# Row sums placed ten rows per head by one-hot weights, and the DMA chain to the softmax broadcast cut from nine transfers to three

## The chip, the cores and the metric

The kernel runs on one core of a Trainium2 chip. The metric is the device time of one execution in microseconds (us). Five engines work side by side, each through its own list of instructions in order: TensorE (PE, matmuls), VectorE (DVE), ScalarE (ACT), GpSimd (POOL) and SyncE (SP, which here only issues DMA transfers). They wait for each other through semaphores.

## What is computed

The reference is an attention in two parts, followed by a dense layer pair with a SiLU between:

```python
# q, k, v: [8 batches, 8 heads, 576, 64]
q_d, k_d, v_d = means of 4 neighbouring rows           # 144 rows
out_up   = repeat(softmax(q_d k_d^T / 8) v_d, 4)       # coarse part
out_local = softmax(q k^T / 8, masked to |i - j| < 4) v # band part
x = (out_up + out_local) reshaped to [4608, 512]
h = x @ w_in                                            # [4608, 2048]
out = (h * sigmoid(h)) @ w_out                          # [4608, 512]
```

Each softmax needs the sum of a row of exponentials and its reciprocal. The change is about how these sums get from TensorE to the place where the attention output is multiplied by them.

## The kernel before

Two heads make a pair; there are 32 pairs. For pair `p` the exponentials lie transposed (keys on partitions, queries along the free axis) in `Pt` (band part, 576 queries) and `Pd` (coarse part, 2 x 72 keys, 144 queries). There are five buffers of each (`NP_ = 5`), four of the broadcast reciprocals `Rb` (`NR = 4`), and two PSUM pairs `duo` for everything that attention does on TensorE.

Pairs 0 to 7 (`direct`) get their reciprocals through matmuls (`ph_ZD`, `ph_RB`). Pairs 8 to 31 use the chain that is changed, two pairs at a time (`z = p // 2`), twelve passes in all:

```python
def ph_Z(z):
    D, bk = next_duo()
    i = z % 2
    ...
    hd = [(32 * (2 * a + h), prs[a] % NP_, h) for a in range(2) for h in range(2)]
    for o, m, h in hd:                       # 4 heads, side by side in 4 column groups
        mm(D[o:o + 32, 0, 0:360], ones_bf[:, 0:32], Pt[m][:, h, 0:360], ...)
    for o, m, h in hd:
        mm(D[o:o + 32, 1, 0:216], ones_bf[:, 0:32], Pt[m][:, h, 360:576], ...)
    for s in range(2):
        for o, m, h in hd:
            mm(D[o:o + 32, 1, 216:360], fours_bf[:, 0:32], Pd[m][:, h, s, :], ...)
    # 720 sums per head, the same in each of 32 rows
    P.op("ACT", lambda e: e.activation(zc[i], D[:, :, 0:360], AF.Copy), ...)          # PSUM -> SBUF
    for o in range(4):                                                              # 4 DMAs
        P.op("SP", lambda s, o=o: s.dma_start(
            zr[i][10 * o:10 * o + 10, :],                     # one row of 720 -> ten of 72
            zsrc[32 * o:32 * o + 1, :].rearrange("p (c n) -> p c n", c=10)), ...)

def do_recip(z):
    P.op("DVE", lambda e: e.reciprocal(rr[i], zr[i]), ...)                            # 40 x 72
    P.op("SP", lambda s: s.dma_start(scr[i].rearrange(...), rr[i]), ...)              # 1 DMA, to DRAM

def do_bcast(z):
    for a in range(2):
        for h in range(2):                                                          # 4 DMAs
            P.op("SP", lambda s: s.dma_start(
                Rb[n][64 * h:64 * h + 64, :],                 # one row of 720 to 64 partitions
                scr[i][2 * a + h:2 * a + h + 1, :].to_broadcast([64, 720])), ...)

def ph_PV(p):
    ...                                                       # 14 matmuls into a duo
    P.op("DVE", ... xo[x][:, 0:456]   = D[:, 0, 0:456] * Rb[u][:, 0:456])
    P.op("DVE", ... xo[x][:, 456:720] = D[:, 1, 0:264] * Rb[u][:, 456:720])
    do_add(p)                                                 # POOL: band + coarse -> xT
```

The dense layers are cut in nine token blocks of 512. A first-layer group `g1` is four matmuls into `hps`, a tanh on ACT (`th`) and a multiply on DVE (`gT`); a second-layer group `g2` is four matmuls into `ops`. There are 144 of each.

The order of all instructions is planned in the program itself, by a list scheduler: every operation is given a duration (`cost`, in ns), every DMA an issue time and a cost on a modelled ring, and the planner takes next what would be ready first. Each engine then executes its list in that fixed order. A changed duration can therefore move instructions anywhere in the kernel.

Of the kernel before, what the change touches and what calls it, by code (L numbers as in the profile page):

```python
# [32 lines left out]
class Op:  # L33
    __slots__ = ("t0", "eng", "fn", "waits", "pos", "K", "inc", "dsem", "dval", "semval", "end")
# [7 lines left out]
class Prog:  # L42
# [9 lines left out]
    def __init__(self):  # L52
        self.streams = {e: [] for e in self.ENGS}
        self.know = {e: {} for e in self.ENGS}
        self.dcount = {}
        self.free = {e: 0 for e in self.ENGS}
        self.rings = {"SP": [], "POOL": [], "ACT": []}
        self.ring_t = 0

# [54 lines left out]
    def op(self, eng, fn, r=(), w=(), dma=None, cost=0):  # L114
        op = Op(eng, fn)
        op.pos = len(self.streams[eng])
        know = self.know[eng]
        deps = []
        for x in r:
            if x.psum:  # L120
                deps += [(o, False) for e, o in x.last.items() if e != eng]
            else:
                deps += [(o, True) for o in x.writers]
        for x in w:
            if x.psum:
                deps += [(o, False) for e, o in x.last.items() if e != eng]
            else:
                rd = x.readers + ([op] if x in r else [])
                if rd:
                    x.prev, x.readers, x.writers = rd + x.writers, [], []  # L130
                deps += [(o, dma is not None or eng != "PE") for o in x.prev]
                if dma is not None:
                    deps += [(o, True) for o in x.writers if o.dsem != dma]
        deps = [(d, f) for d, f in deps if d is not op]
        t = self.free[eng]
        for d, f in deps:
            if d.eng != eng or d.dsem:
                t = max(t, d.end + self.LATENCY[d.eng])
        if dma:
            op.t0 = t  # L140
            t += 450 if eng == "SP" else 650 if eng == "ACT" else 800
            self.free[eng] = max(t, self._dma(op, eng, t, cost * DMA_SLOW) if eng != "POOL" else t)
            if eng == "POOL":
                self._dma(op, eng, t, cost * DMA_SLOW)
        else:
            self.free[eng] = op.end = t + cost * (2 if eng == "PE" and t < 30000 else 1)
        deps.sort(key=lambda df: -(df[0].pos if not df[0].dsem else 1 << 30))
        for d, f in deps:
            self._dep(op, d, know, f)
        op.waits = [  # L150
            w for w in op.waits
            if not any(v is not w and v[2].K.get(w[0], -1) >= w[1] for v in op.waits)
        ]
        for x in r:
            if x.psum:
                x.last[eng] = op
            elif x not in w:
                x.readers.append(op)
        for x in w:
            if x.psum:  # L160
                x.last[eng] = op
            else:
                x.writers.append(op)
        op.K = dict(know)
        if dma:
            self.dcount[dma] = self.dcount.get(dma, 0) + 16
            op.dsem, op.dval = dma, self.dcount[dma]
            op.K[dma] = op.dval
        else:
            op.K[eng] = op.pos  # L170
        self.streams[eng].append(op)
        return op
# [36 lines left out]
def bass_hourglass_attn__then__act_silu_kernel(  # L209
# [9 lines left out]
    with kctx:  # L219
# [40 lines left out]
        zc = sb("zc", [128, 2, 360], F32, 2)  # L260
        zr = sb("zr", [40, 72], F32, 2)
        rr = sb("rr", [40, 72], F32, 2)
        Rb = sb("Rb", [128, 720], F32, NR)
        xo = sb("xo", [128, 720], F32, 2)
        scr = [nc.dram_tensor(f"scr{i}", [4, 720], F32, kind="Internal").ap() for i in range(2)]
# [3 lines left out]
        ones_bf = sb("ones_bf", [128, 64], BF16)  # L269
        fours_bf = sb("fours_bf", [72, 64], BF16)  # L270
# [23 lines left out]
        def const_g():  # L294
            pool(lambda g: g.memset(ones_bf[:, :], 1.0), w=[R("ones")])
            pool(lambda g: g.memset(fours_bf[:, :], 4.0), w=[R("ones")])
# [41 lines left out]
        def load_T(p, x):  # L338
            j = p % 2
            src, dst = (qb, qr) if x == "q" else (kb, kr)  # L340
            P.op("SP", lambda e: e.dma_start_transpose(
                dst[j][:, :, :], src[j][:, :, :, :].rearrange("p c h d -> p (c h d)")),
                r=[R(f"{x}b{j}")], w=[R(f"{x}r{j}")], dma=f"{x}r{j}", cost=700)
            P.free["SP"] += 700

        def order_T(p, x):
# [3 lines left out]
            if x == "q":  # L350
                P.op("DVE", lambda e: e.tensor_copy(dst, src), r=[R(f"qr{j}")], w=[R(f"qT{y}")], cost=700)
            else:
                P.op("ACT", lambda e: e.activation(dst, src, AF.Copy), r=[R(f"kr{j}")], w=[R(f"kT{y}")], cost=700)  # L353

        def load_v(p):
# [3 lines left out]
            for hh in range(2):  # L359
# [4 lines left out]
                     w=rs_, dma=sem, cost=900)  # L364
            if p in direct:
# [3 lines left out]
                 w=[R(f"vq{i}")], dma=f"vq{i}", cost=870)  # L369
            P.op("SP", lambda s: s.dma_start(vq[i][64:72, :, :], src[64:72]),  # L370
                 w=[R(f"vq{i}")], dma=f"vq{i}", cost=150)
# [104 lines left out]
        def chain(z):  # L476
            return "SP"

        def ph_Z(z):
# [5 lines left out]
            for o, m, h in hd:  # L485
                mm(D[o:o + 32, 0, 0:360], ones_bf[:, 0:32], Pt[m][:, h, 0:360], rr_, [bk[0]],
                   cost=40, m="col4")
            for o, m, h in hd:
                mm(D[o:o + 32, 1, 0:216], ones_bf[:, 0:32], Pt[m][:, h, 360:576], rr_, [bk[1]],
                   cost=24, m="col4")  # L490
            for s in range(2):
                for o, m, h in hd:
                    mm(D[o:o + 32, 1, 216:360], fours_bf[:, 0:32], Pd[m][:, h, s, :], rr_, [bk[1]],
                       start=(s == 0), stop=(s == 1), cost=16, m="col4")
            P.op("ACT", lambda e: e.activation(zc[i][:, :, :], D[:, :, 0:360], AF.Copy),
                 r=bk, w=[R(f"zc{i}")], cost=770)
            zsrc = zc[i][:, :, :].rearrange("p a n -> p (a n)")
            for o in range(4):
                P.op(chain(z), lambda s, o=o: s.dma_start(  # L499
                    zr[i][10 * o:10 * o + 10, :], zsrc[32 * o:32 * o + 1, :].rearrange("p (c n) -> p c n", c=10)),  # L500
                    r=[R(f"zc{i}")], w=[R(f"zr{i}")], dma=f"zr{i}", cost=100)

        def do_recip(z):
            i = z % 2
            P.op("DVE", lambda e: e.reciprocal(rr[i][:, :], zr[i][:, :]), r=[R(f"zr{i}")], w=[R(f"rr{i}")],
                 cost=600)
            P.op(chain(z), lambda s: s.dma_start(
                scr[i].rearrange("h (c n) -> (h c) n", c=10), rr[i][:, :]),
                r=[R(f"rr{i}")], w=[R(f"scr{i}")], dma=f"scr{i}", cost=100)

        def do_bcast(z):
            i = z % 2
            for a in range(2):
                n = (2 * z + a) % NR
                for h in range(2):
                    P.op(chain(z), lambda s, a=a, h=h, n=n: s.dma_start(
                        Rb[n][64 * h:64 * h + 64, :],
                        scr[i][2 * a + h:2 * a + h + 1, :].to_broadcast([64, 720])),
                        r=[R(f"scr{i}")], w=[R(f"Rb{n}")], dma=f"Rb{n}", cost=500)
# [26 lines left out]
        def const_neg():  # L546

            t = zc[1][:, 0, 0:32].rearrange("p (a g) -> p a g", a=2)
            for a in range(2):
                pool(lambda g, a=a: g.memset(t[:, a, :], -1.0), w=[R("zc1")])  # L550
                for sign, base in ((1, -1 - a), (-1, 7)):
                    pool(lambda g, a=a, sign=sign, base=base: g.affine_select(
                        out=t[:, a, :], in_=t[:, a, :], compare_op=ALU.is_ge, fill=0.0, base=base,
                        pattern=[[-8 * sign, 16]], channel_multiplier=sign), r=[R("zc1")], w=[R("zc1")], cost=120)
            P.op("DVE", lambda e: e.tensor_reduce(neg[:, :], t, mybir.AxisListType.X, ALU.add),
                 r=[R("zc1")], w=[R("neg")], cost=120)
# [22 lines left out]
        def ph_ZD(p):  # L579
# [8 lines left out]
            for s in range(4):  # L588
                for t in range(2):
# [10 lines left out]
            P.op("DVE", lambda e: e.tensor_copy(b0, f0), r=rf, w=rb, cost=150)  # L600
            P.op("DVE", lambda e: e.scalar_tensor_tensor(f1, b0, neg[:, 0:1], f0, ALU.mult, ALU.add),
                 r=rf + rb + [R("neg")], w=rf, cost=150)
            P.op("DVE", lambda e: e.tensor_copy(b1, f1), r=rf, w=rb, cost=150)
            P.op("DVE", lambda e: e.scalar_tensor_tensor(b2, b1, neg[:, 1:2], f1, ALU.mult, ALU.add),
                 r=rf + rb + [R("neg")], w=rb, cost=150)
# [136 lines left out]
        def nm(k, p):  # L742
# [8 lines left out]
            (f"dm{x}", lambda x=x: const_d(x)) for x in range(6)]  # L751
# [5 lines left out]
        for p in range(NPAIR):  # L757
# [34 lines left out]
            elif p % 2 == 1:  # L792
                task(side, f"r{z}", "DVE", [f"Z{z}"], [R(f"zr{z % 2}")], [], lambda z=z: do_recip(z))
                task(side, f"b{z}", chain(z), [f"r{z}", nm("PV", p - 1 - NR), nm("PV", p - NR)],
# [20 lines left out]
            elif p % 2 == 1:  # L815
                task(attn, f"Z{z}", "PE", [f"k{p - 1}", f"k{p}"],
# [18 lines left out]
        def run_side(now, horizon):  # L835

            nxt, again = None, True
            while again:
                again, nxt = False, None
                for t in side[:90]:  # L840
# [4 lines left out]
                    if tm <= now + horizon:  # L845
                        side.remove(t)
                        done.add(t[0])
                        t[5]()
# [35 lines left out]
        const_g()  # L884
        done.add("ones")
        while attn or side or g2n[0] < 16 * NSUP:
# [10 lines left out]
            if ready:  # L897
# [3 lines left out]
                done.add(t[0])  # L901
                t[5]()
                last = t[0]
            elif mready:
# [6 lines left out]
                else:  # L911
                    want = mready[0][1]
                run_mlp(want)
# [43 lines left out]
```

## Time and profile before

The median of 3 runs is 409.66 us (409.6 to 410.45). The profiled execution has a span of 409.0 us and a mean granted TensorE clock of 0.966 of full speed.

| Chain to the broadcast, per pass of two pairs | instructions | duration of one (us) |
|---|---|---|
| copy `zc<-duo` on ACT (L495) | 1 | 0.77 |
| DMA `zr<-zc`, issue on SP (L499) | 4 | 0.73 (median) |
| reciprocal on DVE (L505), 40 x 72 | 1 | 0.59 |
| DMA `scr<-rr`, issue on SP (L507) | 1 | 0.36 (median) |
| DMA `Rb<-scr`, issue on SP (L516), 180 KB each | 4 | 0.60 (median), 4.0 from issue to landing |

How to read the page: PE is TensorE's matmuls and PEld its weight loads, which overlap them; SPq is SP's queue of DMA issues. Rows of 40 digits cut the span in 40 equal slices; a digit is a busy share in tenths, and in the row PEclk the granted clock in tenths. L499 is line 499 of the program. The chain of waits starts at the last instruction and goes back, at each step, to what released it. In a table by stretches, each engine's busy us stand beside the stretch's length, with the number of instructions in brackets; behind them stand the granted clock, the mean busy share of the 16 DMA engines, and GB/s. In a timeline, a line is start, length, engine, source line and instruction, and in square brackets the idle time before it with what ended it.

### The profile page before, as it was taken

What the parts mean: (1) busy time and instruction counts of PE and PEld (TensorE: products, weight loads), DVE (VectorE), ACT (ScalarE), POOL (GpSimd) and SP (SyncE); (2) the same over time, 40 slices, a digit from 0 to 9 for tenths busy, and PEclk for the clock granted to TensorE, in tenths of its full rate; (3) what the DMA queues carried; (4) which work ended last, traced back from release to release, by engine and by line L of the source; (5) the groups of instructions that cost most, each with busy time, mean ns of one, the idle gap of its engine ahead of it and who ended that gap; (6) DMA issues with size and microseconds to landing.
All of it is one profiled execution on the core that took longest, in us unless ns stands there. A gap on an engine that the chain in (4) does not pass through costs nothing.

```text
span 409.0 us, 7353 instructions
## 1 busy us (share of the span) xinstructions
PE 350.3 (86%) x2891; PEld 210.9 (52%) x2928; DVE 245.0 (60%) x391; ACT 224.9 (55%) x379; POOL 161.6 (40%) x211
## 2 busy tenths in 40 slices
PE   2566977869999888779886998889998989999996
PEld 1445745536655455435542665446545555555552
DVE  3958756965777846657477577347775663343320
ACT  4564645718666783648661975455865334344331
POOL 7953713267316643960375406832614220000000
PEclk9999798989999989999988999989999999999999
DMA  8999799567787888997989886979871501101012
GB/s 222 240 315 275 130 217 208 126 155 178 170 240 154 216 194 187 220 184 188 224 210 189 192 164 191 196 194 248 149 214 57 133 14 41 38 27 51 26 53 77
DMA packets 97082, 66.50 MB, mean 163 GB/s; under 512 B 66072, under 2 KB 87320, under 8 KB 97048
## 3 DMA queue, kind: packets, MB, share of 16 engines
q1 hardware_dynamic: 92824, 59.74, 65.2%
q0 software_dynamic: 4224, 6.29, 6.9%
q8 instruction: 23, 0.38, 0.4%
q14 instruction: 11, 0.09, 0.1%
HBM read 53.67 MB, written 9.58 MB: 155 GB/s over the span
## 4 chain that ended last, share of the span: by engine, by line
PE 48%; DMA 13%; DVE 11%; SPq 10%; ACT 7%; POOL 7%; issue 3%; POOLq 0%; ACTq 0%
PE ops L413 21%; PE hps L413 20%; PE duo L413 6%; DMA vs<-in_v_dram 5%; SPq L499 3%; DMA Rb<-scr 3%; DVE gT L688 3%; ACT th L686 2%; DMA vq<-in_v_dram 2%; SPq L363 2%; DVE Pt L471 2%; ACT Pt L448 1%; DMA zr<-zc 1%; DMA kr<-kb 1%; PE duo L423 1%
## 5 line engine op out<-in xcount | busy, mean ns | idle before, releaser
L413 PE MATMUL hps<-xT,w_in_sb 128*128 128x512 f32 x576 | 175.3, 436 | 16.9 <-DVE gT L688 16.8
L688 DVE SCALAR_TENSOR_TENSOR gT<-th,hps 128x512 bf16<-128x512 f32 x144 | 97.8, 685 | 107.9 <-ACT th L686 107.5
L413 PE MATMUL ops<-w_out_bf,gT 128*128 128x512 bf16 x539 | 138.0, 385 | 5.0 <-issue 2.5
L413 PEld LDWEIGHTS hps<-xT,w_in_sb 128*128 128x128 f32 x576 | 107.9, 196 | 54.7 <-DVE gT L688 27.0
L686 ACT ACTIVATE th<-hps 128x512 f32<-128x512 f32 x144 | 85.2, 598 | 78.9 <-PE hps L413 78.5
L413 PEld LDWEIGHTS ops<-w_out_bf,gT 128*128 128x128 bf16 x576 | 48.5, 99 | 69.5 <-issue 21.8
L663 POOL TENSOR_TENSOR xT<-xo 128x576 fp32r<-128x576 f32 (+2 forms) x40 | 41.4, 1048 | 101.8 <-DVE xo L646 101.8
L385 POOL CAST qb<-qs 96x768 bf16<-96x768 f32 x28 | 25.2, 902 | 56.7 <-DMA qs<-in_q_dram 43.0
L448 ACT ACTIVATE Pt<-duo 128x912 bf16<-128x912 f32 x32 | 29.7, 928 | 12.6 <-PE duo L413 12.5
L707 ACT ACTIVATE osb<-ops 128x512 f32<-128x512 f32 x36 | 21.5, 598 | 27.1 <-PE ops L413 27.1
L394 POOL TENSOR_TENSOR vt<-vq 72x512 f32<-72x512 f32 x24 | 31.9, 1329 | 4.5 <-DMA vq<-in_v_dram 3.4
L390 ACT ACTIVATE vb<-vs 128x640 bf16<-128x640 f32 x30 | 21.8, 734 | 21.5 <-DMA vs<-in_v_dram 20.1
L471 DVE TENSOR_TENSOR Pt<-Pt,mask_bf 128x1152 bf16<-128x1152 bf16 x32 | 30.3, 949 | 5.4 <-ACT Pt L463 5.4
L644 DVE TENSOR_TENSOR xo<-duo,Rb 128x456 f32<-128x456 f32 x32 | 20.0, 624 | 12.3 <-DMA Rb<-scr 9.3
L385 POOL CAST kb<-ks 96x768 bf16<-96x768 f32 x28 | 24.1, 860 | 2.2 <-DMA ks<-in_k_dram 2.1
L413 PE MATMUL duo<-qT,kT 64*128 64x112 bf16 (+1 forms) x320 | 18.4, 230 | 7.0 <-DVE xo L644 3.0
L435 DVE TENSOR_REDUCE kd<-kT 128x144 bf16<-128x576 bf16 x32 | 23.7, 740 | 1.0 <-ACT kT L353 1.0
L435 DVE TENSOR_REDUCE qd<-qT 128x144 bf16<-128x576 bf16 x32 | 23.8, 745 | 0.5
L353 ACT ACTIVATE kT<-kr 128x576 bf16<-128x576 bf16 x16 | 19.3, 1206 | 7.9 <-DMA kr<-kb 7.9
L413 PEld LDWEIGHTS duo<-qT,kT 64*128 64x128 bf16 x320 | 10.7, 101 | 21.5 <-issue 8.3
L465 ACT ACTIVATE Pd<-duo 72x576 bf16<-72x576 f32 x32 | 20.7, 646 | 0.0
L396 POOL TENSOR_TENSOR vd<-vt 72x256 bf16<-72x256 f32 x24 | 18.7, 780 | 1.9
(68 smaller groups left out, 263.5 us busy)
## 6 DMA issues: line engine op xcount, KB each, us to landing
vs<-in_v_dram SPq DMA_DIRECT2D x60, 160.0 KB, 5.1
out_dram<-osb SPq DMA_DIRECT2D x36, 256.0 KB, 2.5
qs<-in_q_dram SPq DMA_DIRECT2D x30, 288.0 KB, 4.7
ks<-in_k_dram SPq DMA_DIRECT2D x30, 288.0 KB, 5.4
Rb<-scr SPq DMA_DIRECT2D x48, 180.0 KB, 4.0
vq<-in_v_dram SPq DMA_DIRECT2D x24, 256.0 KB
w_in_sb<-in_moe_w_in_dram POOLq DMA_DIRECT2D x4, 1024.0 KB, 11.4
w_out_bf<-in_moe_w_out_dram POOLq DMA_DIRECT2D x4, 512.0 KB, 8.8
```

The costliest lines, as they stand in the source:

```text
L385: pool(lambda g, d=dst, s=src: g.tensor_copy(d, s), r=rs_, w=[R(f"{nm}b{j}")], cost=830)
L390: P.op("ACT", lambda e: e.activation(vb[m][:, :, :], t, AF.Copy), r=rs_, w=[R(f"vb{m}")], cost=730)
L394: pool(lambda g: g.tensor_tensor(vt[:, :, :], vq[i][:, :, 0:128], vq[i][:, :, 128:256], ALU.add), r=[R(f"vq{i}")], w=[R("vt")], cost=1290)
L413: return P.op("PE", lambda t: t.matmul(out_, lhsT, rhs, start=start, stop=stop, skip_group_check=True), r, w, cost=cost)
L435: P.op("DVE", lambda e: e.tensor_reduce(dst[j][:, :], src[y][:, :].rearrange("p (g r) -> p g r", r=4), mybir.AxisListType.X, ALU.add), r=[ ...
L448: P.op("ACT", lambda e: e.activation(Pt[m][:, :, 0:456], D[:, :, 0:456], AF.Exp, scale=0.125), r=bk, w=[R(f"P{m}")], cost=930)
L465: P.op("ACT", lambda e: e.activation(Pd[m][:, :, :, :].rearrange("p h s n -> p h (s n)"), D[0:72, :, 120:408], AF.Exp, scale=0.0078125), r ...
L471: P.op("DVE", lambda e: e.tensor_tensor(Pt[m][:, :, :], Pt[m][:, :, :], mask_bf[:, :].unsqueeze(1).to_broadcast([128, 2, S_]), ALU.mult), ...
L663: P.op("POOL", lambda e, dst=dst, in0=in0, in1=in1: e.tensor_tensor(dst, in0, in1, ALU.add), r=[R(f"xo{x}")], w=xblk(kc, t, e_), cost=200 ...
L686: P.op("ACT", lambda e: e.activation(th[tb][:, :], hps[hb][:, :], AF.Tanh, scale=0.5), r=[R(f"h{hb}", True)], w=[R(f"th{tb}")], cost=600)
L688: P.op("DVE", lambda e: e.scalar_tensor_tensor(gT[j % 2][:, f, :], th[tb][:, :], 1.0, hps[hb][:, :], ALU.add, ALU.mult), r=[R(f"h{hb}", Tr ...
L707: P.op("ACT", lambda e: e.activation(osb[s_][:, :], ops[ob][:, :], AF.Copy, scale=0.5), r=[R(f"o{ob}", True)], w=[R(f"osb{s_}")], cost=600)
```

## The change

The aim is a shorter way from the row sums to the broadcast. TensorE now puts the 720 sums of a head into ten rows of 72 at once: for block `c` of 72 queries the weights have ones only in column `c` (and its repeats), so that the sums land in row `c` and zeros are added to the others. The reciprocal can then read PSUM directly with 72 columns; the ACT copy and the four rearranging DMAs go. The broadcast's four DMAs become two, each for one head of both pairs. The planner's durations are also changed, for DMA issues, transposes, the copy to `kT` and some DVE operations. The core of the diff:

```diff
-        zc = sb("zc", [128, 2, 360], F32, 2)
-        zr = sb("zr", [40, 72], F32, 2)
-        rr = sb("rr", [40, 72], F32, 2)
-        Rb = sb("Rb", [128, 720], F32, NR)
+        rr = sb("rr", [128, 72], F32, 2)
+        Rbz = sb("Rb", [128, 2, 720], F32, NR // 2)
+        Rb = [Rbz[u // 2][:, u % 2, :] for u in range(NR)]
-        scr = [... [4, 720] ...]
+        scr = [... [128, 72] ...]
-        ones_bf, fours_bf (two memsets on POOL, at the start)
+        onesZ = sb("onesZ", [128, 10, 32], BF16)   (two memsets, two selects on POOL, after the other constants)
...
 def ph_Z(z):
-            for o, m, h in hd: mm(D[o:o + 32, 0, 0:360], ones_bf[:, 0:32], Pt[m][:, h, 0:360], ...)
-            ... (16 matmuls in all)
-            P.op("ACT", ... zc ...)
-            for o in range(4): P.op(SP, ... zr ... DMA)
+            for c in range(12):
+                for o, m, h in hd:
+                    y, t = (c, 0) if c < 8 else (8 + (c - 8) // 2, c % 2)
+                    lhsT, rhs = ((onesZ[:, y, :], Pt[m][:, h, 72 * c:72 * c + 72]) if c < 8 else
+                                 (onesZ[0:72, y, :], Pd[m][:, h, t, 72 * (y - 8):72 * (y - 8) + 72]))
+                    mm(D[o:o + 32, 0, 0:72], lhsT, rhs, rr_, bk[0:1], start=(c == 0), stop=(c == 11), ...)
+            P.op("DVE", lambda e: e.reciprocal(rr[i][:, :], D[:, 0, 0:72]), ...)
 def do_bcast(z):
-            for a in range(2):
-                for h in range(2): ... one DMA of [64, 720]
+            for h in range(2):
+                src = bass.AP(tensor=scr[i].tensor, offset=scr[i].offset + 32 * 72 * h,
+                              ap=[[0, 64], [64 * 72, 2], [1, 720]])
+                P.op("SP", ... dma_start(Rbz[i][64 * h:64 * h + 64, :, :], src), ..., cost=1100, issue=650)
...
 planner's figures (ns)
-  every DMA issue on SP: 450; transpose: 700 on the ring and 700 of SP
+  issue 400 (scr), 550 (vs), 670 and 500 (vq), 650 (Rb), 1250 (transpose, ring 950); others 450
-  kT copy 700; the four small DVE operations of ph_ZD: 150 each
+  kT copy 1210; those four: 210, 314, 210, 314
```

## Prediction

> **What bounds the kernel now.** I read the page first: parts 1, 2 and 4, for which engine is full, when, and what the chain that ended last is made of.
>
> ```profile
> span 409.0 us, 7353 instructions
> PE 350.3 (86%) x2891; PEld 210.9 (52%) x2928; DVE 245.0 (60%) x391; ACT 224.9 (55%) x379; POOL 161.6 (40%) x211
> ...
> PE   2566977869999888779886998889998989999996
> ...
> PEclk9999798989999989999988999989999999999999
> DMA  8999799567787888997989886979871501101012
> ...
> PE 48%; DMA 13%; DVE 11%; SPq 10%; ACT 7%; POOL 7%; issue 3%; POOLq 0%; ACTq 0%
> PE ops L413 21%; PE hps L413 20%; PE duo L413 6%; DMA vs<-in_v_dram 5%; SPq L499 3%; DMA Rb<-scr 3%; DVE gT L688 3%; ACT th L686 2%; DMA vq<-in_v_dram 2%; SPq L363 2%; DVE Pt L471 2%; ACT Pt L448 1%; DMA zr<-zc 1%; DMA kr<-kb 1%; PE duo L423 1%
> ```
>
> PE is the fullest engine, but only 48% of the chain is PE. Of the rest, 23% is DMA flight and the SP queue that issues DMAs, and 3% is one issuing line, L499, the four small copies `zr<-zc`. Slices of 6 to 8 in the PE row sit mostly in the first 60% of the span, while the DMA row shows 8 and 9. So the kernel has three stages, and busy time by stretches gives their sizes:
>
> ```profile
> core 0: us, PE busy (x) PEld busy (x) DVE busy (x) ACT busy (x) POOL busy (x), PEclk, DMA share, GB/s
> 100.00:140.00 40.00, 38.88 (x362) 22.65 (x367) 30.21 (x44) 26.60 (x46) 19.06 (x22) 1.00 0.86 203
> 140.00:180.00 40.00, 32.02 (x236) 18.79 (x240) 25.85 (x44) 23.00 (x37) 23.09 (x23) 0.96 0.91 195
> 180.00:220.00 40.00, 32.85 (x227) 19.39 (x230) 25.97 (x39) 25.16 (x40) 16.35 (x19) 0.93 0.95 204
> 220.00:260.00 40.00, 37.15 (x288) 21.62 (x290) 25.96 (x42) 25.63 (x42) 17.64 (x19) 0.99 0.83 183
> ...
> 340.00:409.00 69.00, 65.54 (x289) 36.95 (x292) 21.29 (x31) 24.58 (x42) 0.00 (x0) 1.00 0.12 46
> ```
>
> From 340 us on only the MLP is left and PE is full, at 0.93 us per group of four hps matmuls and 0.88 us per group of four ops matmuls (the chain's pieces there). The change can't shorten that work. The first 100 us hold pairs 0 to 7, which are `direct` and never use the changed chain; PE is idle there about 29 us, which I leave as it is. What can move is 100 to 340 us, where the other 24 pairs run: PE idle of 1.1, 8.0, 7.1 and 2.9 us in the four stretches shown, and by the same table 2.9 in 260 to 300 and 3.7 in 300 to 340: **25.7 us**. The granted clock also dips there. In 20 us stretches it is 0.91, 0.86, 0.97 and 0.91 (from 140, 200, 220 and 260 us), so 20 x (0.09 + 0.14 + 0.03 + 0.09) = **7.0 us** of PE time. Together 32.7 us can be had at most.
>
> Why PE idles there: the chain from the row sums to the broadcast. Its last pass, in the timelines of ACT, SP and DVE (start, length, instruction):
>
> ```profile
> 313.19 0.77 ACT L495 ACTIVATE zc<-duo 128x720 f32<-128x720 f32 x1 [0.63 <-PE duo L413]
> 313.98 2.99 SPq L499 DMA_DIRECT2D zr<-zc  x4
> ...
> 319.07 0.58 DVE L505 RECIPROCAL rr<-zr 40x72 f32<-40x72 f32 x1
> 320.52 0.52 SPq L507 DMA_DIRECT2D scr<-rr  x1
> 323.48 2.36 SPq L516 DMA_DIRECT2D Rb<-scr  x4
> 328.83 0.62 DVE L644 TENSOR_TENSOR xo<-duo,Rb 128x456 f32<-128x456 f32 x1
> ```
>
> It takes 15.6 us, though there is little else on the SP queue by then. Measured in the same way for all twelve passes (start of L495 to start of the first L644 of its two pairs) it is 15.6 to 31.8 us, mean 23.5. The matrices of a pair are held in one of five `Pt` buffers until its PV matmuls, so this latency limits how fast pairs follow each other (the last 24 take 126 to 329 us, 8.5 us each). And the SP queue runs in order: from 120 to 280 us it is busy 36.9, 38.2, 37.7 and 32.4 us of each 40, by its timeline. L499 alone takes 48 x 0.73 = 35 us of it, and the loads of later pairs stand behind it.
>
> **What the Trainium skill says.** "DMA: Bandwidth & Descriptors", Anatomy of one DMA, says that a small DMA's fixed cost is mostly waiting for confirmation that its last byte has landed. The trace agrees: `scr<-rr` moves 11.2 KB, and 320.52 to 323.48 pass before the dependent issue, 3.0 us. The same page, Latency and other measured facts, says that memory latency grows under load; one 2.8 KB `zr` copy issued at 198.00 took 5.5 us on the chain, with DMA at 0.95 share. "TensorE: Matmul & The Clock Gate", The HAM clock gate, ties the clock to how busy PE has been; the trace has the lower clock (0.86) in 200 to 220 us, where PE is busy 13.5 of 20 us, so part of the 7.0 us should come back with the idle time. Its remark that small matmuls cannot start closer together than about 25 ns does not bind here: `ph_ZD`'s 48 matmuls, packed four across the array, took 44.35 to 44.95 us, 12.5 ns each.
>
> **The change part by part**, each over 12 passes.
> - ACT: the `zc` copy goes, 12 x 0.77 = 9.2 us. ACT is 55% busy; off the path, except as 0.8 us of each latency.
> - SP: 48 `zr` issues go (35 us), 24 of the 48 `Rb` issues go (24 x 0.60 = 14 us), and the larger ones left may cost a little more. I take **-48 us** of issue time, 20% of the 240 us stage.
> - DVE: the reciprocal stays, now 128x72 from PSUM. L599 does 128x90 from PSUM in 716 ns, 8.0 ns a column, so 72 columns are 0.57 us against 0.59 now: nothing.
> - PE: 16 matmuls of a pass become 48 of 72 columns. Now a pass lasts 0.49 us (104.49 to 104.98); the first 16 of `ph_ZD`, the same shape, took 0.23 us, so 48 take 0.69: **+0.2 us, 2.4 us in all**, on the path.
> - DMA bytes: the broadcast still writes 720 KB a pass; `scr` grows from 11 to 36 KB. DMA engine load stays.
> - POOL: building `onesZ` costs about 1 us near 20 us; needed only after 100 us.
> - Latency of a pass: reciprocal 0.6, `scr` issued to landed 3.0, second `Rb` issue 0.6 and its landing 4.0 (median): **8.2 us against 15.6** in the least loaded pass, so 7 us less at least, and more where four `zr` issues now queue.
> - Order: the new order of instructions is planned with issue times and durations near those measured here (1.25 us per transpose, 1.21 for the kT copy). Its PE stream has 112 hps and 101 ops groups ahead of the last PV against 107 and 98, and 5 + 6 groups between the last row sums and that PV, 5 x 0.93 + 6 x 0.88 = 9.9 us, enough to cover 8.2. The tail after the PV shrinks from 37 x 0.93 + 46 x 0.88 = 74.9 to 67.6 us. That only moves work; it gains when the gaps it fills were idle.
>
> **The sum.** By the table of waits DVE stood idle for `Rb` 9.3 us and for `zr` 6.6 us, and PE's largest wait in this stage (11.5 us, hps on gT) is for DVE, whose queue is in order behind those. 15.9 us is about half of the 32.7, and half (16.3) is what I choose: the other half belongs to q, k and v loads, casts and two-deep PSUM buffers, which stay. Less 2.4 for PE's added work: 13.9. 409.7 - 13.9 = **396 us**.
>
> **The rivals.**
> 1. *DMA takes over.* Its share is 0.83 to 0.95 from 100 to 300 us, with the same bytes to move. If 190 to 200 GB/s is all that these 256-byte pieces allow, a free SP queue only waits for a full ring. For it: single `vs` issues of over 3 us. Against: 0.86 at 100 to 140 us, and 203 GB/s beside 297 at 20 to 40 us. Only the last pass, which no load follows, would then be shorter, by 7 us: about 403.
> 2. *PE becomes the bound everywhere.* All 32.7 recovered, less 2.4: 379. The five `Pt` buffers and the casts behind loads (POOL waits 43 us for `qs`) speak against it.
> 3. *The new order collides.* A whole new order, in-order queues, and the reciprocal holding a PSUM pair until DVE comes to it. PE would show new waits on rr, and the time be 405 to 412 (nothing won, and PE's added 2.4 us lost). Against: its durations fit this trace better than the old ones.
>
> **Range and chances.** Between rival 1 and a recovery of three quarters of the 32.7 lies 387 to 405. The 2% line is at 401.5 us, 5.5 above my figure: three chances in four to be beyond it, and few for a loss.
>
> **What would show it.** Right: row sums to first `xo` of about 10 to 15 us on average; SP busy below 32 us per 40; PE idle in 100 to 340 us below 15; the clock nearer 1.00 there; last PV near 325 us or earlier. Wrong: DMA share pinned at 0.95 or more with `vs` or `qs` waits larger; PE waiting on rr; a first 100 us that the new order has made longer; or latency halved with PE idle unchanged, in which case loads and not this chain set the pace.

## The result, and the profile after

The changed kernel takes **394.75 us** (median of 4 runs, 390.6 to 396.44) against 410.06 (4 runs, 409.6 to 410.74): the ratio is 0.961, with a 95% interval of 0.953 to 0.969. Forecast were 396 us and 387 to 405. The profiled run is the longest of the four, 396.44 us. Its page, parts 1, 2 and 4:

```profile
span 394.7 us, 8030 instructions
PE 346.1 (88%) x3272; PEld 213.9 (54%) x3312; DVE 248.7 (63%) x391; ACT 217.6 (55%) x367; POOL 162.6 (41%) x213
...
PE   2658886959999979998999999999979999999996
...
PEclk9999696968999997999999999999989999999999
DMA  8999699865596599999999999999983031000012
...
PE 60%; DMA 12%; DVE 11%; ACT 7%; POOL 5%; issue 3%; SPq 2%; POOLq 0%; ACTq 0%; DVEq 0%
```

PE holds 60% of the chain that ended last, 48% before; the SP queue fell from 10% to 2%, and DMA flight stayed at 12%. The span is 14.3 us shorter; in PE's two parts that is idle time, 58.7 to 48.6 us (-10.1), and busy time, 350.3 to 346.1 (-4.2). Busy time by stretches, columns as in the table before:

```profile
core 0: us, PE busy (x) PEld busy (x) DVE busy (x) ACT busy (x) POOL busy (x), PEclk, DMA share, GB/s
...
100.00:140.00 40.00, 38.31 (x438) 23.82 (x445) 30.94 (x46) 25.30 (x45) 20.90 (x25) 1.00 0.71 177
140.00:180.00 40.00, 35.82 (x355) 22.57 (x357) 30.18 (x49) 27.30 (x44) 22.49 (x23) 0.91 1.19 206
180.00:220.00 40.00, 37.85 (x348) 22.68 (x351) 28.35 (x44) 26.41 (x42) 20.54 (x22) 1.00 1.17 226
220.00:260.00 40.00, 38.82 (x353) 22.88 (x358) 28.45 (x42) 25.41 (x42) 22.90 (x26) 1.00 1.15 230
260.00:300.00 40.00, 35.87 (x329) 21.34 (x334) 28.16 (x44) 25.58 (x42) 16.88 (x16) 0.96 1.01 199
300.00:340.00 40.00, 38.83 (x274) 24.71 (x278) 20.07 (x32) 16.98 (x30) 4.75 (x4) 1.00 0.17 53
340.00:394.70 54.70, 50.78 (x223) 28.25 (x225) 16.51 (x24) 19.43 (x33) 0.00 (x0) 1.00 0.12 44
```

From 140 to 220 us PE is now busy 35.8 and 37.9 us of 40, where it was 32.0 and 32.9. Over 100 to 340 us its idle time fell from 25.7 to **14.5 us**. Some records of PE are missing in these traces (539 and 536 of the 576 `ops` matmuls are there) and count as idle: the same order with all 576, in the last experiment, shows 10.4 us. The DMA share rose from 0.83 to 0.95 to about 1.15 over 140 to 260 us. The first 100 us gave nothing (idle 29.5, now 30.2), and the clock in 40 to 100 us was lower in this run, 0.80 against 0.89.

The last pass of the chain, in the timelines of DVE and SP:

```profile
312.41 0.60 DVE L498 RECIPROCAL rr<-duo 128x72 f32<-128x72 f32 x1
313.72 0.43 SPq L502 DMA_DIRECT2D scr<-rr  x1
315.57 1.23 SPq L510 DMA_DIRECT2D Rb<-scr  x2
...
322.97 0.63 DVE L636 TENSOR_TENSOR xo<-duo,Rb 128x456 f32<-128x456 f32 x1 [1.73 <-PE duo L421]
```

10.6 us from the reciprocal to the first `xo`, of 15.6 before; the bracket says that this `xo` waited last for PE, not for the broadcast. Over all twelve passes the mean is 17.8 us against 23.5. In the table of waits, from longest to shortest, these lines belong to the chain and to what stands behind it (who waited, for whom: us, times, longest):

```profile
PEld hps L421 <- DVE gT L680: 11.5, 15, 4.2
...
PE hps L421 <- DVE gT L680: 7.2, 7, 4.0
...
DVE xo L636 <- DMA Rb<-scr: 4.2, 3, 2.8
```

DVE stood idle for the chain's DMAs for 15.9 us before (`Rb` 9.3, `zr` 6.6), and for 4.2 now. PE's wait for `gT` fell from 16.8 to 7.2 us.

### The profile page after: what moved, and what is told of

It reads as the page before. It is cut to its first block, busy times and chain, and to the rows that moved or that the text cites. A ratio compares the mean times of both kernels' runs of the same rounds, so it can differ in the third digit from the quotient of the medians.

```text
span 394.7 us, 8030 instructions
## 1 busy us (share of the span) xinstructions
PE 346.1 (88%) x3272; PEld 213.9 (54%) x3312; DVE 248.7 (63%) x391; ACT 217.6 (55%) x367; POOL 162.6 (41%) x213
## 4 chain that ended last, share of the span: by engine, by line
PE 60%; DMA 12%; DVE 11%; ACT 7%; POOL 5%; issue 3%; SPq 2%; POOLq 0%; ACTq 0%; DVEq 0%
PE hps L421 28%; PE ops L421 24%; PE duo L421 7%; DMA Rb<-scr 4%; DMA vs<-in_v_dram 4%; ACT th L678 3%; DVE gT L680 2%; DVE xo L636 2%; DMA qr<-qb 2%; DMA kr<-kb 2%; DVE Pt L479 1%; DVE gT L593 1%; DVE xo L638 1%; ACT Pt L456 1%; DMA scr<-rr 1%
## 5 line engine op out<-in xcount | busy, mean ns | idle before, releaser
L421 PE MATMUL hps<-xT,w_in_sb 128*128 128x512 f32 x576 | 173.5, 435 | 7.2 <-DVE gT L680 7.2
L421 PE MATMUL ops<-w_out_bf,gT 128*128 128x512 bf16 x536 | 140.8, 390 | 7.2 <-issue 4.0
L421 PEld LDWEIGHTS hps<-xT,w_in_sb 128*128 128x128 f32 x576 | 109.2, 195 | 40.0 <-DVE gT L680 11.5
L655 POOL TENSOR_TENSOR xT<-xo 128x576 fp32r<-128x576 f32 (+2 forms) x40 | 40.4, 1032 | 108.4 <-DVE xo L638 108.4
L393 POOL CAST qb<-qs 96x768 bf16<-96x768 f32 x28 | 24.0, 856 | 39.0 <-DMA qs<-in_q_dram 25.0
L402 POOL TENSOR_TENSOR vt<-vq 72x512 f32<-72x512 f32 x24 | 33.2, 1384 | 8.8 <-DMA vq<-in_v_dram 8.0
L404 POOL TENSOR_TENSOR vd<-vt 72x256 bf16<-72x256 f32 x24 | 19.5, 814 | 1.9
```

The lines of the kernel that those rows point to most:

```text
L393: pool(lambda g, d=dst, s=src: g.tensor_copy(d, s), r=rs_, w=[R(f"{nm}b{j}")], cost=830)
L402: pool(lambda g: g.tensor_tensor(vt[:, :, :], vq[i][:, :, 0:128], vq[i][:, :, 128:256], ALU.add), r=[R(f"vq{i}")], w=[R("vt")], cost=1290)
L421: return P.op("PE", lambda t: t.matmul(out_, lhsT, rhs, start=start, stop=stop, skip_group_check=True), r, w, cost=cost)
L655: P.op("POOL", lambda e, dst=dst, in0=in0, in1=in1: e.tensor_tensor(dst, in0, in1, ALU.add), r=[R(f"xo{x}")], w=xblk(kc, t, e_), cost=200 ...
```

## The experiments

The theories: **L**, the latency of the chain costs time, because engines with lists in fixed order stand behind what waits for it; **Q**, the issue time of the SP queue did it, 48 us less; **F**, the planner's new figures did it; **D**, DMA bandwidth bounds the stage now. All ratios are to the kernel before, run on the same chip; they leave out executions more than 1.5% above the fastest of their kernel, which the medians and ranges include.

### The old chain with the planner's new figures

```diff
 kernel before
-  issue 450 for all, transpose 700 + 700, kT 700, ph_ZD 150
+  the new figures; zr issue=730, scr issue=400, Rb issue=600
```

> The kernel before with its nine-DMA chain, and the planner's new figures (its zr issues planned at 0.73 us, scr 0.40, Rb 0.60, as measured). Theory L (the latency of the chain sets the pace of the pairs): the chain is as long as before, so 404 to 410 us. Theory Q (issue time of the SP queue): the 35 us of zr issues are still there, so 404 to 410. Rival theory F (the planner's figures and the order that follows from them did it): 394 to 399.

Measured: **422.39 us**, ratio 1.026 (1.020 to 1.033), slower by 12 us. F falls in its plain form. The passes are as long as before (mean 23.4 us), and what the figures did is another order of PE: its list differs from the old one in many places, the last PV stands behind 112 hps and 108 ops groups instead of 107 and 98, and the last `xo` starts at 352.8 us instead of 329.7. In its table of waits:

```profile
PE hps L412 <- DVE gT L687: 12.9, 18, 2.0
PE duo L412 <- DVE xo L643: 12.1, 7, 5.5
...
PE duo L412 <- DVE Pt L470: 6.9, 5, 3.1
```

PE stands 12.1 us for `xo` to free a PSUM pair, 5.5 us in one case; it was 5.4 in all before. Why true durations make a worse order for the long chain is not settled; the planner chooses greedily, and nothing here tells which of its choices cost it.

### The new chain with the old figures

```diff
 changed kernel
-  the new figures
+  issue 450 for all, transpose 700 + 700, kT 700, ph_ZD 150
```

> The changed kernel with the planner's old figures (450 ns for every issue, 700 for transposes and the kT copy, 150 for the small DVE operations). Theories L and Q: the new chain works under any order, 395 to 400 us. Theory F: the order is planned on wrong durations again, 404 to 410.

Measured: **399.26 us**, ratio 0.971 (0.966 to 0.977). The chain alone wins 2.9% under the old figures, and PE idle from 100 to 340 us is 14.2 us, with no record missing. The figures may add another 1%; the intervals overlap, so that is not clear of noise.

### New sums, four broadcast DMAs; and old sums, two

```diff
 changed kernel
-  2 DMAs of [64, 2, 720], each for one head of both pairs
+  4 DMAs of [64, 720]; each pair waits for its own two
```

> The changed kernel, but the broadcast goes out as four DMAs of 180 KB instead of two of 360 KB; each pair waits only for its own two. Adds 24 issues of 0.6 us, 14 us of SP time. Theory L: the first pair's data may even land earlier, 393 to 397 us. Theory Q: 14 of the 48 us of issue time are back, about 4 us longer, 397 to 401.

Measured: 395.12 us, ratio 0.962 (0.958 to 0.966), the same as with two. The four land in 4.5 us (median), the two in 6.8, and the mean pass is 16.1 us: what the merged broadcast saves in issues it gives back in flight.

> The old row sums with the ACT copy and four zr DMAs, but the broadcast as two DMAs, with the new figures. Removes 14 us of SP issue time and 1.2 us of latency per pass against the run with the old chain and the new figures. Theory L: within 2 us of that run. Theory Q: 3 to 5 us below it. Theory F: the same as that run, near 396.

Measured: 421.61 us, ratio 1.025 (1.019 to 1.031), the same as the first experiment. Merging the broadcast is worth nothing that can be measured on either side; the one-hot sums are the change.

### One more hop in the chain

```diff
-  SP: scr[i] <- rr[i]
+  SP: pre[i] <- rr[i]          # DRAM
+  SP: scr[i] <- pre[i]         # DRAM to DRAM, 36 KB
```

> The changed kernel with one more small DMA in the chain: the reciprocals go to a second DRAM buffer first and from there to the one that is broadcast (36 KB, 0.4 us of issue each, 12 in all; the planner knows of it). Adds 3 to 5 us of latency per pass and only 5 us of SP issue time. Theory L (latency of the chain): the passes are 18 us now and were 23.5 before for 15 us of time, so 3 to 5 us of latency cost 7 to 12 us: 402 to 407. Theory Q (SP issue time): 395 to 397.

Measured: **404.77 us**, ratio 0.985 (0.980 to 0.989). The mean pass is 23.0 us, as in the kernel before, and 10 of the 15 us are lost, with only twelve small issues more. But the planner knew of the hop and made another order: PE's list leaves that of the changed kernel at 126 us, and 109 hps and 97 ops groups stand ahead of the last PV instead of 112 and 101. The 10 us are therefore the price of the latency together with the order planned for it; no run adds the hop in the changed kernel's order. Its waits:

```profile
PEld hps L422 <- DVE gT L686: 27.4, 28, 5.1
PE hps L422 <- DVE gT L686: 18.6, 16, 5.0
...
DVE xo L642 <- DMA Rb<-scr: 11.0, 5, 3.8
```

DVE waits 11.0 us for `Rb` (4.2 in the changed kernel), and PE 18.6 us for `gT` (7.2). DVE's list is in order, so it is tempting to read the second as caused by the first. The timelines of PE, DVE and ACT at PE's longest stall after 100 us show something else:

```profile
168.65 0.73 PE L422 MATMUL hps<-xT,w_in_sb 128*128 128x512 f32 x2 [2.74 <-DVE gT L686]
...
167.91 1.28 DVE L686 SCALAR_TENSOR_TENSOR gT<-th,hps 128x512 bf16<-128x512 f32 x2 [1.05 <-ACT th L684]
...
166.65 0.74 ACT L399 ACTIVATE vb<-vs 128x640 bf16<-128x640 f32 x1 [2.40 <-DMA vs<-in_v_dram]
167.29 1.07 ACT L684 ACTIVATE th<-hps 128x512 f32<-128x512 f32 x2
```

ACT stood for a v load, with the tanh behind it in its list. The next stall (1.75 us at 149.89) goes back to a DVE copy that waited for a q transpose; the longest that goes back to `Rb` is the eighth, 0.86 us at 278.90. The table follows every idle stretch of PE over 0.15 us, from 100 to 340 us, in this way, to the first DMA or PE instruction that ended a wait (us):

| PE's idle time goes back to | before | changed | extra hop |
|---|---|---|---|
| the chain's `Rb` and `zr` | 7.2 | 2.2 | 2.0 |
| v loads, q and k transposes | 6.9 | 2.9 | 9.7 |
| PE's own earlier matmuls | 8.1 | 5.1 | 5.9 |
| nothing that the trace shows | 1.9 | 3.0 | 1.7 |

What the hop lost stands in the second row. SP's list is in order as well, and SP stands 12.6 us for the hop to land (3.3 for the store in the changed kernel), but none of this falls between 130 and 260 us, where the loss is: PE idles 16.0 us from 140 to 260 us, 7.5 in the changed kernel. That speaks for the new order as what made PE wait for loads; it is not shown.

### Issue time without latency

```diff
+  for o in range(4):                                  # behind the broadcast, each pass
+      SP: zo[10 * o:10 * o + 10] <- zi[32 * o]        # zeros; nothing reads zo
```

> The changed kernel with four small copies per pass like the old zr copies, from a tile of zeros to a tile that nothing reads, issued behind the broadcast (planned at 0.73 us each): 35 us of SP issue time come back, the chain gets no new step. Theory Q: 35 of the 48 us are back, so 403 to 408. Theory L: 395 to 399, only what the later loads feel.

Measured: 404.37 us, but 397.0 to 405.9 over four runs, ratio 0.973 (0.962 to 0.984). The planner had made another order of it (112 hps and 112 ops groups ahead of the last PV), so this told nothing about SP. The copies again, planned as free, with the order of all engines kept:

> The changed kernel with the four idle copies per pass behind the broadcast, as in the earlier run, but planned as if they cost nothing, so that every engine keeps the order of the changed kernel and only SP has 48 issues of 0.7 us more. Theory Q (SP issue time): 400 to 406. Theory L: 394 to 398. If it stays near 395, the 404 of the earlier run came from the order that the planner made of them.

Measured: **398.46 us**, ratio 0.972 (0.968 to 0.976). 35 us of issue time cost about 4 us, between the ranges of L and Q. The interval just touches that of the changed kernel (0.953 to 0.969) and is clear of the second series with a sixth buffer, which has the same order (0.954 to 0.964). From the first to the last `xo` of the chain the profiled runs show the same 4 us: 200.6, against 196.7. Q is real but small, perhaps a quarter of the gain. This is the only addition that was tried in a fixed order.

### Less to load, and the chain on another queue

```diff
-  if p in direct: return                  # load_v
+  if p in direct or p >= 10: return       # no vq loads from pair 10 on
```

> The changed kernel without the vq loads from pair 10 on (the coarse v then comes from stale rows, so this computes something else): 22 x 288 KB less to move of 66.7 MB, 44 issues less on SP, about 26 us. Rival theory D (DMA is what bounds the stage now, its share is 1.15 from 140 to 260 us): 383 to 389. Theory L: the chain's DMAs land a little sooner, 390 to 394. If neither DMA nor SP matters any more: 394 to 396.

Measured: 394.40 us, ratio 0.957 (0.950 to 0.964), not told apart from the changed kernel. Here the coarse `v` from pair 10 on comes from rows loaded earlier. In the profiled runs attention ended far earlier, by the last `xo` start of 309.0 us against 323.9 in the changed kernel (instructions of tile `xo`: duration min/median/max, first and last start):

```profile
L636 DVE TENSOR_TENSOR xo<-duo,Rb x32: 620/624/633, 25.3 to 309.0; 128x456 f32<-128x456 f32 x32
```

```profile
L636 DVE TENSOR_TENSOR xo<-duo,Rb x32: 622/626/634, 25.3 to 323.9; 128x456 f32<-128x456 f32 x32
```

Of these 15 us, about 5 are spread: where the two lists of PE part, one run is at 105.1 us and the other at 110.2, and a lead of 6 us is there at 70 us already, before the first load that is left out. (The run profiled here took 390.84 us, that of the changed kernel 396.44, the longest of its four.) The other 10 us bought nothing that the medians show; PE then has a longer MLP tail, and its idle time from 100 to 340 us is 13.0 us instead of 14.5. D falls as the bound of the total time: removing 6.3 MB and 44 issues changed it by nothing that can be measured, though the DMA share had risen above 1. The loads do set part of attention's own pace: from the first to the last `xo` of the chain it took 188.7 us, against 196.7.

> The changed kernel with the three DMAs of the chain issued from ACT instead of SP (planned at the planner's 650 ns for ACT). Removes 20 us from SP and, from the chain, the waits behind other issues: 3.0 us from reciprocal to its store on average, where the issue itself needs 0.1. Theory L: 388 to 393 if ACT is free when the store has landed. Against it: ACT runs in order, and stands still while it waits for the store to land, some 3 us in each pass, which would make it 397 to 404.

Measured: 398.96 us, 394.6 to 403.1, ratio 0.967 (0.956 to 0.977). The mean pass fell to 15.5 us and the last `xo` came some 10 us earlier (a difference that the changed kernel's order alone also shows from run to run, see the sixth buffer), but the time did not fall; whether ACT's own waits cost it, the runs don't tell.

### A sixth buffer

```diff
-  NVB, NP_ = 5, 5
+  NVB, NP_ = 5, 6       # Pt and Pd (in the kernel before also one zc buffer, to make room)
```

> The kernel before with six Pt and Pd buffers instead of five (and one zc buffer instead of two, to make room). The long chain stays. Theory L with the buffers (each pair holds a Pt buffer through the chain, so five buffers and 23.5 us set the pace): a sixth buffer lets one more pair run ahead and wins most of what the change won, 396 to 402. If the buffers are not what ties the latency to the time: 407 to 411.

Measured: 410.26 us, ratio 1.001 (0.999 to 1.003). PE's order is that of the kernel before, instruction for instruction: the planner never lacked a sixth `Pt` buffer.

> The changed kernel with six Pt and Pd buffers instead of five. Theory L with the buffers: some gain is left, 386 to 391. If the buffers are not the link, or PE's own work now bounds: 393 to 397.

Measured: 390.90 us, ratio 0.953 (0.946 to 0.960), again in an unchanged PE order. Since this overlaps with 0.961 (0.953 to 0.969), it was run again:

> The changed kernel with six Pt and Pd buffers a second time, in more rounds. Its order of instructions on PE is that of the changed kernel, instruction for instruction, so the sixth buffer can only take waits away at run time. If the 390.9 us of the first time is the buffer's gain: ratio to before 0.945 to 0.957, 388 to 392. If it was the spread of the runs: 0.957 to 0.967, 393 to 397.

Measured: 395.81 us, ratio 0.959 (0.954 to 0.964). The sixth buffer gains nothing that two series agree on, and the 390.9 was mostly spread. The two profiled runs, with one order on every engine, show where it arises: their spans are 386.8 and 396.1 us, and the same `gT` multiply starts at 64.0 and 71.4 us, so 7.3 of the 9.3 us are there while the first eight pairs run, before the chain is used at all. The last `xo` of the two starts at 315.9 and 325.2 us, which is how far a single run's last `xo` can be trusted. No version here is shown to beat the changed kernel.

## Why the prediction was right, and where its steps were not

- **The sum came out close, in part by luck.** Of the 16.3 us of idle and clock time that were to come back, the profiled runs show 13.0: PE idle in 100 to 340 us fell by 11.2 (below the 15 that the forecast named as a sign), and the clock's loss there, by 20 us stretches, from 7.0 to 5.2. PE's added work was 0.2 instead of 2.4. The two errors offset each other: 12.8 us against 13.9. The span fell by 14.3, because PE's busy time fell by 4.2 as well, less 1.1 us more of idle time outside 100 to 340 us. The 4.2 us had no place in the forecast and are not explained; the clock of the whole run was lower, 0.957 against 0.966.
- **What is shown of the cause, and what is not.** The new sums win under both sets of figures (0.971 against 1, and 0.961 against 1.026), with two broadcast DMAs or four. Which of their effects does it is shown only for SP's issue time, about a quarter. The rest is the shorter way together with the order that the planner makes for it; nor was the copy on ACT, or the time that a PSUM pair is held for it, tried alone.
- **The reason for the half: right in direction, argued in size.** It was taken from DVE's 15.9 us of waiting for the chain and PE's waiting behind DVE. This path is in the trace of the kernel before, in the timelines of DVE and PE:

```profile
203.55 0.60 DVE L505 RECIPROCAL rr<-zr 40x72 f32<-40x72 f32 x1 [4.50 <-DMA zr<-zc]
204.07 0.69 DVE L471 TENSOR_TENSOR Pt<-Pt,mask_bf 128x1152 bf16<-128x1152 bf16 x1
204.68 0.73 DVE L435 TENSOR_REDUCE kd<-kT 128x144 bf16<-128x576 bf16 x1
205.33 0.67 DVE L688 SCALAR_TENSOR_TENSOR gT<-th,hps 128x512 bf16<-128x512 f32 x1
...
206.06 0.50 PE L413 MATMUL hps<-xT,w_in_sb 128*128 128x512 f32 x1 [2.80 <-DVE gT L688]
```

  But only 7.2 us of PE's idle time went back to the chain, and 5.0 of them were won, less than half of the 11.2; waits for loads and transposes, which the forecast had counted as staying, fell by 4.0, and those for PE itself by 3.0. Nor does DVE's waiting measure the loss: the run with four idle copies in the planner's own order shows DVE waiting 13.6 us for `Rb` and PE 17.4 us idle, the run with the extra hop 11.0 and 21.3. One profile of each kernel stands behind this.
- **"This latency limits how fast pairs follow each other", through the five `Pt` buffers: wrong.** The sixth buffer left the order of PE untouched and the time as it was. And with passes of 23.0 us instead of 17.8, the run with the extra hop took as long from the first to the last `xo` of the chain, 196.6 us against 196.7. What moved was the MLP work that PE did beside them.
- **The clock** gave back 1.8 of the 7.0 us. That the lower clock goes with idle time does not come out of these runs: with the extra hop PE idled 21.3 us, and the clock was 1.00 in each 20 us from 100 to 340.
- **The latency after was mis-sized.** Least loaded pass 10.6 us, forecast 8.2; mean 17.8, forecast 10 to 15. The terms were the landings: `Rb` 6.8 us in median (taken as 4.0, from pieces half the size) and 4.5 for `scr` (taken as 3.0). Of the 8.4 us from sums to reciprocal that went, 2.9 came back between the `Rb` issue and `xo`. The wait from reciprocal to the `scr` issue stayed, 2.9 and 3.0 us. What the 3.0 us between the `scr` issue and the dependent one are spent on, no run shows.
- **SP: -48 us of issue time was right, "below 32 us per 40" wrong.** From 160 to 280 us SP is busy 37.2, 37.6 and 38.1 us of each 40. Other issues became longer, so that all of SP's issues together fell by 29 us, from 248.1 to 219.1; what holds them was not tried. Two of them in the timeline of SP:

```profile
203.54 3.71 SPq L350 DMA_TRANSPOSE qr<-qb  x1
...
230.62 3.15 SPq L371 DMA_DIRECT2D vs<-in_v_dram  x2
```

  3.71 us for a transpose that mostly needs 1.25, and 3.15 for two `vs` issues that need 1.1. So SP's busy time was no measure of its work.
- **PE's added work: about 0.2 us, forecast 2.4.** The 48 matmuls of a pass took 0.51 us to the start of the next work (110.19 to 110.70 in PE's timeline), the old sixteen 0.49; times twelve, 0.2 us. The forecast scaled from sixteen matmuls of `ph_ZD` that ran at a granted clock of 0.50 (44 to 45 us); those of the new sums here had 1.00.
- **DVE 0.60 us a reciprocal from PSUM (0.57 forecast), ACT and POOL off the path:** as forecast.
- **The last PV and the tail:** `xo` at 323.9 us ("near 325 or earlier"), within the spread; then 70 us to the end instead of 78, where 67.6 and 74.9 had been counted from the order.
- **Rival 1, DMA,** showed its sign, a share pinned above 0.95, and still wasn't the bound: waits for `qs` fell from 43.0 to 25.0 us, and taking loads away won nothing. **Rival 3, the order,** did not strike the changed kernel, but the first experiment shows how strong it is: figures alone moved the old chain by 12 us. "Its durations fit this trace better" was no argument for a better order.

## What to carry to other kernels

A chain of small DMAs can cost time through an engine that isn't busy: look in the table of waits for an in-order engine that stands for the chain's last transfer, and at what stands behind it in the same list. Then follow the stalls of the fullest engine back one by one, because two waits that grow together need not be one path. To tell latency from issue time, add each alone with the order of instructions held fixed; here only the issues were added so. In a planned kernel, compare orders first; a change of planning figures can outweigh the change that is studied. And compare the start of two runs before their ends: here up to 7 us of difference arose before the changed code ran.

## What was not expected of the hardware

Packed four across the array, 32 matmuls of 72 columns were spaced 0.27 us in all (110.19 to 110.46), 8.4 ns each, at full clock. The store of 36 KB to DRAM took 1.8 to 7.5 us to land, median 4.5, most of them under a DMA share near or above 1; the broadcasts of 360 KB took 4.3 to 9.2. And the mean busy share of the DMA engines, about 1.15 from 140 to 260 us, was not what bounds the total time: with 6.3 MB less it was 1.01 there, and the time was the same. So a share near 1 alone doesn't show that a kernel's time is bound by DMA.
